# A fused linear attention and highway layer on one core: one written list of steps in place of a list scheduler, with the bias laid into PSUM by ScalarE and part of the blend on GpSimd

## The chip, the cores and the metric

The kernel runs on one core of one Trainium2 chip. The metric is the device time of one execution in microseconds (us), lower is better. Every time is a median of several executions; executions of one kernel mostly agree within a few per cent, and a run over 1.5% above the fastest of the same kernel is set aside as slow. A ratio is the mean time of one kernel's fast runs over the mean of the other kernel's fast runs of the same rounds on the same chip, so it is not quite the ratio of the medians quoted beside it; its 95% interval follows in brackets. The engines are TensorE (PE in the profile; its weight loads, PEld, run beside it), VectorE (DVE), ScalarE (ACT), GpSimd (POOL) and SyncE (SP), which here only issues transfers.

## The reference, cut to what matters

```python
# q, k, v: (8 batches, 8 heads, 576 rows, 64), float32; weights 512x512; output (4608, 512)
q_s = exp(q - max(q, -1));  q_s = q_s / sum(q_s, -1)        # softmax along the head dimension
k_s = exp(k - max(k, 2));   k_s = k_s / sum(k_s, 2)         # softmax along the sequence
kv  = einsum('bhsd,bhse->bhde', k_s, v)                     # 64x64 for each head
att = einsum('bhsd,bhde->bhse', q_s, kv)
x   = att.transpose(0, 2, 1, 3).reshape(4608, 512)
H   = maximum(x @ w_h, 0)
T   = sigmoid(x @ w_t + b_t)
out = T * H + (1 - T) * x
```

## The kernel before

Tokens go through in 36 tiles of 128 rows, four or five to a batch. For each batch: exponentials of k and q (ScalarE), casts of v, the product K'V (36 small matmuls per batch), its division by the sums, and transposes of exp(q) whose copies out of PSUM ("eq") feed the next product. For each tile: `xu` (product of eq and K'V), `x` (the division, VectorE), `xt` and `xe` (transposing x and copying it to SBUF), `mt` and `mh` (four 512-column matmuls each against the two weight matrices), `th` (tanh, ScalarE), `dd` and `uu` (the blend, VectorE), `oo` (the last addition, GpSimd) and two stores. w_h is halved and half of the identity taken from it beforehand, so that `mh` gives (x w_h - x)/2 and the blend is d = max((x w_h - x)/2, -x/2) and out = (tanh + 1) d + x, with tanh of half the T product.

What the change touches:

```python
    def mt(i, n, cols):                       # T product: four matmuls and a fifth for the bias
        ...
        if n < 4:
            nc.tensor.matmul(ps, T[f"xT{i}"][:, n], wt16[:, n, cols], start=(n == 0), stop=False,
                             skip_group_check=True)
        else:
            nc.tensor.matmul(ps, ones, b16[:, cols], start=False, stop=True, skip_group_check=True)
    ...
    def uu(i, cols):
        ...
        nc.vector.scalar_tensor_tensor(
            T[f"u{i}"][:, cols], T[f"tps{i}"][:, cols], 1.0, T[f"d{i}"][:, cols], op0=ALU.add, op1=ALU.mult)

    def oo(i, cols):
        ...
        eng = nc.vector if i == last else nc.gpsimd
        eng.tensor_add(T[f"o{i}"][:, cols], T[f"u{i}"][:, cols], T[f"x{i}"][:, cols])
    ...
    def wcast_h(c):                           # gate weights, on GpSimd in four pieces
        nc.gpsimd.tensor_scalar_mul(wh16[:, c], T["w32h"][:, c], 0.5)
```

All steps are entered into a list scheduler with an assumed length for each kind; it simulates the engines, buffers and loads and emits the instructions in the order that comes out.

The softmax here doesn't subtract the row's maximum and nothing guards it: scores larger than these inputs give would overflow.

## Time and profile before

The time was 137.18 us (136.13 to 138.89, 3 runs).

| engine | busy us of 134.7 | share |
|---|---|---|
| TensorE | 118.4 | 88% |
| VectorE | 104.4 | 77% |
| ScalarE | 88.5 | 66% |
| GpSimd | 63.1 | 47% |

TensorE idles 0.24 us between 40 and 121 us. Three more lines, from the groups of instructions by line and shape, are used later. The columns are line, engine, operation, output and input, shapes, count, then busy time in us and the mean of one in ns, then the idle time before them and what ended it:

```profile
L551 POOL TENSOR_TENSOR o<-u,x 128x512 f32<-128x512 f16 x35 | 40.4, 1155 | 43.9 <-DVE u L544 29.3 <-DMA out_dram<-o 5.1 <-DVE rz L402 4.6
...
L544 DVE SCALAR_TENSOR_TENSOR u<-tps,d 128x512 f16<-128x512 f32 x35 | 24.1, 688 | 2.8 <-ACT xT L515 0.5
...
L525 PE MATMUL tps<-b,ones 128*128 128x512 f16 x35 | 13.5, 386 | 0.0
```

All full-size output additions are on GpSimd at 1155 ns, VectorE's part of the blend takes 688 ns, and the bias matmul shows 386 ns.

The K'V products are good milestones, since there is one per batch and TensorE runs them in order. Three of them in the timeline of before (start us, length, engine, line, operation):

```profile
44.04 1.21 PE L391 MATMUL kv<-v,ek 64*128 64x130 f16 x36
67.06 1.21 PE L391 MATMUL kv<-v,ek 64*128 64x130 f16 x36
105.53 1.21 PE L391 MATMUL kv<-v,ek 64*128 64x130 f16 x36
```

### The profile page before, as it was taken

Reading aid. Unit: us, or ns where it says so; the run is one execution under the profiler, and the core shown is the slowest. Engines: PE = TensorE matmul, PEld = TensorE weight load, DVE = VectorE, ACT = ScalarE, POOL = GpSimd, SP = SyncE. Lnnn points to the kernel's source line nnn. Section 1 sums busy time; section 2 is a strip of 40 time slices with the busy share of each in tenths; the row PEclk is TensorE's granted clock in tenths of the full one; section 3 lists DMA queues with packets and bytes.
Section 4 is the critical chain, followed back from the end, with each engine's and each line's share of the span. In section 5 each row is a group of like instructions: output and inputs, shape, how many; then the busy total and the mean of one; then the engine's idle time right before and its main releaser. Section 6 shows DMA issues by size and latency. Waiting matters only on the chain.

```text
span 134.7 us, 3213 instructions
## 1 busy us (share of the span) xinstructions
PE 118.4 (88%) x1179; PEld 73.4 (55%) x1179; DVE 104.4 (77%) x220; ACT 88.5 (66%) x131; POOL 63.1 (47%) x63
## 2 busy tenths in 40 slices
PE   4778758879599999999999999999999999999920
PEld 4666533536255656665666575656665756555500
DVE  5566535999869798878989897879898977996760
ACT  3345464478885997979857979977697467444320
POOL 3011049536374349428833682495339516435430
PEclk9999986999999999999999999999999999999995
DMA  3999999999999999999999999999993341223234
GB/s 72 377 391 386 374 370 392 380 387 365 337 389 400 392 399 400 394 332 367 336 321 361 318 406 399 267 361 356 404 379 143 140 94 74 85 87 144 86 130 104
DMA packets 21011, 40.05 MB, mean 297 GB/s; under 512 B 1922, under 2 KB 4226, under 8 KB 20996
## 3 DMA queue, kind: packets, MB, share of 16 engines
q1 hardware_dynamic: 20832, 39.72, 82.5%
q8 instruction: 9, 0.15, 0.5%
q10 hardware_dynamic: 164, 0.14, 0.4%
q14 instruction: 6, 0.05, 0.1%
HBM read 30.41 MB, written 9.44 MB: 296 GB/s over the span
## 4 chain that ended last, share of the span: by engine, by line
PE 67%; DMA 15%; DVE 7%; POOL 5%; issue 2%; SPq 1%; DVEq 0%; POOLq 0%
PE tps L522 21%; PE gps L530 19%; DMA w32h<-in_moe_w_h_dram 10%; PE kv L391 6%; PE xu L491 6%; PE qps L445 5%; PE xtps L509 5%; PE tps L525 5%; DMA q<-in_q_dram 3%; POOL wh L326 3%; DVE u L544 2%; POOL o L551 2%; DMA out_dram<-o 2%; DVE x L502 2%; DVE d L539 1%
## 5 line engine op out<-in xcount | busy, mean ns | idle before, releaser
L551 POOL TENSOR_TENSOR o<-u,x 128x512 f32<-128x512 f16 x35 | 40.4, 1155 | 43.9 <-DVE u L544 29.3
L522 PE MATMUL tps<-wt,xT 128*128 128x512 f16 (+1 forms) x148 | 38.7, 379 | 1.4 <-ACT xT L515 0.8
L530 PE MATMUL gps<-wh,xT 128*128 128x512 f16 x144 | 38.2, 381 | 1.6 <-DVE wh L330 0.9
L515 ACT COPY xT<-xtps 128x512 f16<-128x512 f16 (+1 forms) x37 | 21.1, 571 | 15.6 <-PE xtps L509 15.5
L534 ACT ACTIVATE tps<-tps 128x512 f32<-128x512 f32 (+1 forms) x37 | 21.2, 572 | 12.2 <-PE tps L525 10.0
L544 DVE SCALAR_TENSOR_TENSOR u<-tps,d 128x512 f16<-128x512 f32 (+1 forms) x37 | 24.8, 674 | 3.7 <-ACT tps L534 1.0
L502 DVE TENSOR_TENSOR x<-xu,rs 128x512 f16<-128x512 f32 (+1 forms) x37 | 25.1, 678 | 3.3
L539 DVE SCALAR_TENSOR_TENSOR d<-x,gps 128x512 f16<-128x512 f16 x36 | 24.4, 679 | 2.7 <-PE gps L530 2.7
L374 POOL CAST v<-v 128x1152 f16<-128x1152 f32 (+1 forms) x16 | 16.4, 1026 | 15.0 <-DMA v<-in_v_dram 15.0
L436 ACT ACTIVATE qe<-q 128x1024 f16<-128x1024 f32 (+1 forms) x24 | 20.0, 840 | 3.8 <-DMA q<-in_q_dram 3.7
L366 ACT ACTIVATE ek<-k 128x1152 f16<-128x1152 f32 (+1 forms) x20 | 18.8, 967 | 3.5 <-DMA k<-in_k_dram 3.5
L522 PEld LDWEIGHTS <-xT 128*128 128x128 f16 x148 | 13.0, 99 | 12.5 <-issue 2.8
L530 PEld LDWEIGHTS <-xT 128*128 128x128 f16 x144 | 13.0, 99 | 10.8 <-issue 0.7
L491 PE MATMUL xu<-kvb,eq 128*128 128x130 f16 (+1 forms) x160 | 14.7, 226 | 1.3 <-DVE x L502 1.3
L491 PEld LDWEIGHTS <-eq 128*128 128x128 f16 (+1 forms) x160 | 10.8, 102 | 8.6 <-DVE x L502 3.0
L445 PE MATMUL qps<-idh,qe 128*128 128x128 f16 x144 | 12.2, 221 | 3.4 <-ACT qe L436 3.4
L509 PE MATMUL xtps<-idh,x 128*128 128x128 f16 x144 | 14.3, 221 | 0.2
L509 PEld LDWEIGHTS <-x 128*128 128x128 f16 x144 | 10.6, 98 | 6.7 <-DVE x L502 0.5
L525 PE MATMUL tps<-b,ones 128*128 128x512 f16 (+1 forms) x37 | 14.1, 380 | 0.0
L445 PEld LDWEIGHTS <-qe 128*128 128x128 f16 x144 | 9.4, 99 | 7.3 <-ACT qe L436 4.0
L498 DVE RECIPROCAL rs<-xu 128x8 f32<-128x8 f32 (+1 forms) x37 | 7.6, 204 | 6.8 <-PE xu L491 6.5
L457 ACT COPY eq<-qps 128x1024 f16<-128x1024 f16 x10 | 10.2, 1016 | 1.3 <-PE qps L445 1.3
(36 smaller groups left out, 79.4 us busy)
## 6 DMA issues: line engine op xcount, KB each, us to landing
k<-in_k_dram SPq DMA_DIRECT2D x16, 576.0 KB, 6.6
v<-in_v_dram SPq DMA_DIRECT2D x16, 576.0 KB, 7.7
out_dram<-o SPq DMA_DIRECT2D x70, 128.0 KB, 5.1
q<-in_q_dram SPq DMA_DIRECT2D x6, 1152.0 KB, 9.1
q<-in_q_dram SPq DMA_DIRECT2D x2, 640.0 KB, 12.0
q<-in_q_dram SPq DMA_DIRECT2D x2, 512.0 KB, 8.3
w32t<-in_moe_w_t_dram SPq DMA_DIRECT2D x2, 512.0 KB, 9.0
w32h<-in_moe_w_h_dram SPq DMA_DIRECT2D x2, 512.0 KB, 13.3
```

The lines of the kernel that those rows point to most:

```text
L445: nc.tensor.matmul(ps[:, j - j0, kk], T[f"qe{b}"][:, j, 2 * kk:2 * kk + 2].rearrange("p c d -> p (c d)"), idh, is_transpose=True, start=Tr ...
L491: nc.tensor.matmul(dst, T[f"eq{b}_{jp // 2}"][:, jp % 2, n], kvb[b % NKV][:, half_, kk], start=True, stop=True, skip_group_check=True)
L502: nc.vector.tensor_mul(T[f"xn{i}"][:, k0:k1], z[:, :, :, 0:64], r.unsqueeze(3).to_broadcast([P, k1 - k0, 4, D]))
L509: nc.tensor.matmul(T[f"xtps{i}"][:, n], T[f"x{i}"][:, n * P:(n + 1) * P], idh, is_transpose=True, start=True, stop=True, skip_group_check= ...
L515: nc.scalar.copy(T[f"xT{i}"][:, 2 * k0:2 * k1], T[f"xtps{i}"][:, 2 * k0:2 * k1])
L522: nc.tensor.matmul(ps, T[f"xT{i}"][:, n], wt16[:, n, cols], start=(n == 0), stop=False, skip_group_check=True)
L525: nc.tensor.matmul(ps, ones, b16[:, cols], start=False, stop=True, skip_group_check=True)
L530: nc.tensor.matmul(T[f"gps{i}"], T[f"xT{i}"][:, n], wh16[:, n], start=(n == 0), stop=(n == 3), skip_group_check=True)
L534: nc.scalar.activation(T[f"tps{i}"][:, cols], T[f"tps{i}"][:, cols], AF.Tanh, scale=0.5)
L539: nc.vector.scalar_tensor_tensor(d, T[f"x{i}"], -0.5, T[f"gps{i}"], op0=ALU.mult, op1=ALU.max)
L544: nc.vector.scalar_tensor_tensor(T[f"u{i}"][:, cols], T[f"tps{i}"][:, cols], 1.0, T[f"d{i}"][:, cols], op0=ALU.add, op1=ALU.mult)
L551: eng.tensor_add(T[f"o{i}"][:, cols], T[f"u{i}"][:, cols], T[f"x{i}"][:, cols])
```

## The change

The scheduler goes; a string with every step in order takes its place, and each step may name its engine (`:A` ScalarE, `:D` VectorE, `:P` GpSimd). Within this list: the bias of 26 tiles is copied into PSUM by ScalarE from a tile that holds it on all rows (`ball`), so that the T product adds to it; the product of 12 tiles' blend goes to GpSimd, which then makes two of its operations (`ee`, `uu`), while these tiles' or others' output additions, 12 in all, go to VectorE; w_h is loaded first and cast by VectorE; and tile 4's x is made in two halves as tile 0's was. The cut diff:

```diff
-class Plan:
-    ...                                  # the list scheduler, its lengths and its rules
+ORDER = """
+b_0 b_32 setuppool k_0_0 v_0_0 q_0_0 fill_24 half v_0_2 setupdve k_0_2 w_h_0 q_0_4 w_h_2 bsplit ek_0_0 ek_0_1 ball
+w_t_0 vc_0_1:A vc_0_0:D w_t_2 eq_0_0 v_1_0 fill_35 qt_0_0 kv_0_0 qc_0_0 bw_1 q_1_0 vc_0_2:D ek_0_3 kr_0_0 ek_0_2
+...
+    HALVED = (0, 4)
+...
+    def load_ball(e):
+        nc.scalar.dma_start(ball, moe_b_t.rearrange("(o n) -> o n", o=1).broadcast_to([P, DM]))
+...
+    def wh_cast(e, c):
+        nc.vector.tensor_scalar_mul(w16["h"][:, c:c + 2], w32["h"][:, c:c + 2], 0.5)
+...
+        if e == "A":
+            nc.scalar.copy(t, ball)
+        else:
+            nc.tensor.matmul(t, ones, b16, start=True, stop=False, skip_group_check=True)
+...
+        if lifted(i):
+            T[f"e{i}"] = dp.tile([P, DM], FP16, tag="e16", name=f"e16_{i}")
+            nc.gpsimd.tensor_add(T[f"e{i}"], T[f"d{i}"], T[f"x{i}"])
+...
+        if lifted(i):
+            nc.gpsimd.tensor_mul(t, T[f"th{i}"], T[f"d{i}"])
+        else:
+            nc.vector.scalar_tensor_tensor(t[:, cs], T[f"tps{i}"][:, cs], 1.0, T[f"d{i}"][:, cs],
+                                           op0=ALU.add, op1=ALU.mult)
+...
+        eng = nc.vector if e == "D" or i == LAST else nc.gpsimd
+        eng.tensor_add(t[:, cs], T[f"u{i}"][:, cs], T[f"{'e' if lifted(i) else 'x'}{i}"][:, cs])
```

The intent is to take the bias off the busiest engine, to spread the blend over VectorE and GpSimd, and to fix by hand an order that the scheduler's assumed lengths could not find.

## The prediction

> **What bounds the kernel now.** I read the page first, then the chain that ended last, then stretches of the timeline, to see whether the busiest engine is also the one whose order sets the end. From the page (40 slices of 3.37 us):
>
> ```profile
> span 134.7 us, 3213 instructions
> PE 118.4 (88%) x1179; PEld 73.4 (55%) x1179; DVE 104.4 (77%) x220; ACT 88.5 (66%) x131; POOL 63.1 (47%) x63
> ...
> PE   4778758879599999999999999999999999999920
> ...
> DVE  5566535999869798878989897879898977996760
> ...
> DMA  3999999999999999999999999999993341223234
> GB/s 72 377 391 386 374 370 392 380 387 365 337 389 400 392 399 400 394 332 367 336 321 361 318 406 399 267 361 356 404 379 143 140 94 74 85 87 144 86 130 104
> ```
>
> TensorE is full from slice 12 (40 us) to the tail, VectorE is near full beside it, and the DMA engines are full until about 101 us. The stretch 40 to 121 us, in the order busy PE, PEld, DVE, ACT, POOL, then granted clock, DMA share, GB/s:
>
> ```profile
> 40.00:121.00 81.00, 80.76 (x809) 49.16 (x809) 69.85 (x138) 61.57 (x92) 42.87 (x38) 1.00 0.84 301
> ```
>
> TensorE idles 0.24 us of 81, at full clock; VectorE still has 11.2 us of idle. As the end of a busy TensorE is modelled, I take its real pace from start times in the timeline (start, length, engine):
>
> ```profile
> 100.53 1.03 PE L522 MATMUL tps<-wt,xT 128*128 128x512 f16 x4
> ...
> 101.39 0.38 PE L525 MATMUL tps<-b,ones 128*128 128x512 f16 x1
> ...
> 101.60 0.40 PE L491 MATMUL xu<-kvb,eq 128*128 128x130 f16 x4
> ```
>
> Four 512-column matmuls take 0.86 us, one bias matmul (L525) 0.21 to 0.22 us of TensorE's order, not its 0.38. Before 40 us something else rules. The chain (start, length, what) and one later line of the timeline:
>
> ```profile
> 5.65 13.01 DMA w32h<-in_moe_w_h_dram
> 18.74 4.42 POOL wh L326 x3
> 23.18 0.70 DVE wh L330
> 23.92 0.38 PE gps L530
> ```
> ```profile
> 32.40 0.69 PE L391 MATMUL kv<-v,ek 64*128 64x130 f16 x18
> ```
>
> The gate weights land last, GpSimd casts them at 1491 ns a piece, and TensorE finishes tile 0's H product only after 25 us; batch 1's second K'V is at 32.40 us.
>
> **What the Trainium skill says.** "TensorE: Matmul & The Clock Gate", section "Wait — 56ns, not 53.3ns?", gives 215.7 ns from start to start for warm 512-column matmuls; 0.86 us for four agrees, so I use 0.2157. "PSUM — Partial Sum Buffer", section "The four PSUM rules", says that ScalarE writes neither set nor clear the written bits, and a matmul without the first flag adds where the bit is set. So the copied bias is added to only because the first user of each of the two T banks (tiles 0 and 1) still is a TensorE bias matmul with the flag and no later product has it; the trace of before cannot show this. "SBUF — State Buffer", section "Who interferes with whom", says a VectorE instruction with two SBUF inputs contends with GpSimd's reads. The kernel before has just two such adds, in the tail (418 ns for 256 columns), with GpSimd idle, so it shows nothing; the change makes twelve more beside GpSimd. "VectorE: DVE Perf Modes", section "Mode 2×_2P — use both read ports for one tensor", gives fp32 tensor_scalar in SBUF twice the rate; the casts of v at 746 ns for 576 columns do not show it, the 164 ns of the 128-column scaled identity leaves it possible.
>
> **The change part by part.**
>
> *Bias.* 37 bias matmuls (two of them halves, so 36 full ones' worth) become 10; 26 tiles get a ScalarE copy. TensorE loses 26 x 0.2157 = 5.6 us. The work that TensorE must do, at its real pace: 292 products of T and H worth 288 full ones, 62.2 us; bias 7.8; 36 xu groups 8.8 (32 x 0.23 + 4 x 0.35); 144 transposes of x and 144 of q at 0.056, 16.2; K'V 9.4 (6 x 1.15 + 4 x 0.63). Sum 104.4 before, 98.8 after. TensorE's last matmul ends at 129.2 us, so 24.8 us of that are idle, cold or filling. With that waste unchanged the span would be 134.7 - 5.6 = 129.1.
>
> *Head.* The list loads w_h before w_t, casts both on VectorE in two pieces each (by 576 columns in 746 ns, 1024 take some 1.2 us, or 0.63 if the double rate holds), and does tile 0's H product first. Bytes up to the last weight are the same 5.6 MB plus 0.26 for the bias spread over all rows, so weights are complete near 19.5 us (before 18.7). But tile 0 no longer waits for 5.9 us of GpSimd casts: its blend should come near 23 us (before 28.43). Batch 1's inputs are in after 8.8 MB, at 2.3 + 8.8/0.383 = 25.3 us; its second K'V should run near 28 instead of 32.4. Gain of the head some 4 us, an estimate.
>
> *VectorE.* Out: 12 blends x 0.688 = 8.3. In: 12 output adds x 0.69 = 8.3 (from x at 692 ns, same size). In: xT copies of 6 tiles and two halves, 6 x 0.60 + 2 x 0.28 = 4.1 (interpolated between the 1221 ns and 282 ns PSUM copies). Copies of q: 6 + 8 small become 4 + 6 small, -3.0. Two v casts fewer, -1.5; weight casts +2.5 to 4.8. Net +2 to +5: 104.4 becomes 106 to 109 us.
>
> *ScalarE.* 26 x 0.58 = 15.1 in; 8 steps of xT out, -4.1; q copies +2.7; v casts +3.2; w_t casts -2.1: 88.5 becomes 103.
>
> *GpSimd.* 12 adds of 1.155 and the 5.9 us of weight casts out, 24 new ops (e and u of 12 tiles) at some 1.15 in, v casts -1.8: 63 becomes 69. Not a bound.
>
> *Finer x steps.* Tile 4 is now halved as tile 0 was, and reciprocals stand apart from their products in the list; two more instructions each. This only matters at the start of batch 1 and is in the head's estimate.
>
> **What ends it: three bounds close together.** TensorE with the head's gain: 129.1 - 4 = 125. DMA: the last load of before is a v half issued at 94.38 us, cast by GpSimd at 101.88, and batch 7's K'V starts at 105.53. In the list 36 of the 74 stores stand before the last load (before: 42 of 74), so 30.4 + 0.26 + 36 x 0.131 = 35.4 MB must move first. At 383 GB/s (mean of slices 2 to 17) that is 92 us, at 370 (slices 2 to 30) 96; with 2.4 us to start, the last k lands at 95 to 98, its exponential (1.16 us) and handover bring K'V of batch 7 to 97 to 100. After it the list has 19 products of 4 (16.4 us), 7 xu (1.8), 7 xt (1.6), 12 transposes of q (0.7), one bias and K'V itself (1.4): 21.9 us, say 22.5 with small gaps, and the tail from the last matmul to the end is 5.5 us in before. That makes 125 to 128. VectorE: 107 us of work; it idled 9.3 us in the first 20 and 6.5 us after 121, which little can shorten, and 4 us more must be lost between: 127. With three lists that must mesh at 82 to 86% each, I take a span of 127.7. The median of before lies 2.5 us over its profiled span, so **130.2 us**, 5% less.
>
> **Rivals.** (a) *The bias was hidden, VectorE or the DMA binds and the time stays.* For: VectorE has 8 to 9 tenths nearly everywhere. Against: TensorE's 0.24 us idle in 81, where VectorE had 11 us free. If VectorE keeps those 11 us of idle with 3 us more work, the span is about 134 and the time 136. (b) *The shared SBUF port stretches the 12 adds and GpSimd's 24 ops:* up to one GpSimd op (1.15 us) per add on VectorE is 12 x 1.15 = 14 us at worst, a third of it likely if it happens at all; then near 132 to 134. (c) *A fixed order stalls:* with q, T, H and x buffers of one or two, one late copy on ScalarE (82% busy now) holds TensorE and lets its clock fall, as at 20 to 30 us (0.88). Against: the order looks made for just this, with xu two tiles ahead. Worth +2 us. (d) *The head gains its full 7 us* (TensorE wasted 7.2 us of 20 to 40) and the DMA keeps 395: 127.
>
> **Range and chances.** (d) sets the low end near 126.5, (b) with (c) the high end near 134. Only (a) or the worst of (b) keeps it above 134.4, the line of 2%; 5.6 us off the engine that was full for 81 us speaks strongly against. Faster by over 2%: 0.89; within: 0.10; slower: 0.01.
>
> **What would show it.** Right: 10 bias matmuls and 26 ScalarE copies of some 0.58 us; tile 0's blend near 23 us; K'V of batch 7 at 97 to 100; TensorE's last matmul near 122; VectorE near 107 busy, ScalarE near 103. Wrong: TensorE idle over some 4 us between 40 and 115 us with VectorE named as releaser (a); adds on VectorE or ops on GpSimd well over 0.69 and 1.15 us (b); granted clock under 0.97 after 40 us (c); DMA share well under 0.95 before the last load, so that TensorE waits at K'V.

## The result, and the profile after

The changed kernel took 131.11 us (130.32 to 133.31) against 137.02 for before in the same rounds, a ratio of 0.9589 [0.9502, 0.9676]: 4% faster. The profile read here is that of the control run e0_after, the same kernel again (131.53 us, span 129.7). The lines that answer to those of the page of before:

```profile
span 129.7 us, 3132 instructions
PE 113.2 (87%) x1170; PEld 71.5 (55%) x1170; DVE 105.2 (81%) x228; ACT 100.1 (77%) x156; POOL 71.6 (55%) x69
...
PE   4949379986999989999999999999998999999910
...
DMA  4999999999999999999999979999998450462453
```

TensorE has lost 5.2 busy us, ScalarE has gained 11.6, and TensorE is now full from slice 11 (32 us) on, with dents in slice 15 (45 to 49 us) and slice 31 (97 to 101 us). The DMA row keeps its nines to about 97 us, with one dent in slice 24 (75 to 78 us). The stretch of 40 to 121 us (busy PE, PEld, VectorE, ScalarE, GpSimd, each with its count, then granted clock, DMA share, GB/s), with a part of it:

```profile
40.00:60.00 20.00, 19.19 (x217) 11.79 (x216) 18.26 (x35) 18.95 (x30) 10.33 (x10) 1.00 1.05 390
...
96.00:102.00 6.00, 5.47 (x66) 3.68 (x65) 4.33 (x10) 5.48 (x10) 4.56 (x5) 1.00 0.77 286
...
40.00:121.00 81.00, 79.25 (x801) 47.59 (x800) 72.90 (x144) 74.61 (x117) 59.44 (x50) 1.00 0.85 306
```

TensorE still bounds this stretch, but idles 1.75 us in it where before idled 0.24. Nearly half of that, 0.81 us, lies between 40 and 60 us, where ScalarE is busy 18.95 of 20 us; another 0.53 at 96 to 102 us, around the last K'V. What TensorE waited for in the whole stretch (us in total, times, longest; waits too short to be named are left out):

```profile
PE qps L273 <- ACT eq L282: 0.4, 1, 0.4
PE gps L354 <- ACT xT L332: 0.3, 1, 0.3
PE xu L303 <- ACT eq L282: 0.3, 1, 0.3
PE turned L325 <- DVE x L318: 0.2, 1, 0.2
PE kv L238 <- ACT ek L224: 0.2, 1, 0.2
PE kv L238 <- DVE x L318: 0.2, 1, 0.2
```

So 1.2 us are put down to ScalarE and 0.4 to VectorE. The groups of the moved work:

```profile
L385 POOL TENSOR_TENSOR u<-th,d 128x512 f16<-128x512 f16 x12 | 15.2, 1267 | 1.6 <-ACT th L368 1.6
L338 ACT COPY tps<-ball 128x512 f32<-128x512 f32 x26 | 15.1, 593 | 0.5 <-DVE u L387 0.3
L379 POOL TENSOR_TENSOR e<-d,x 128x512 f16<-128x512 f16 x12 | 14.6, 1218 | 5.8 <-DVE d L374 5.7
...
L394 DVE TENSOR_TENSOR o<-u,x 128x512 f32<-128x512 f16 x6 | 7.0, 1172 | 0.1
...
L394 DVE TENSOR_TENSOR o<-u,e 128x512 f32<-128x512 f16 x6 | 5.4, 893 | 0.7 <-DMA out_dram<-o 0.7
...
L340 PE MATMUL tps<-b,ones 128*128 128x512 f16 x10 | 3.8, 380 | 0.0
```

The counts are as predicted. The additions on VectorE are not: they take 1172 and 893 ns in the mean, not 690. Asked for that line alone, the trace gives for the second of these groups a shortest, middle and longest duration of 684, 690 and 1469 ns. One by one, six of the twelve take 676 to 693 ns and six take 1141 to 1619. What sets them apart: each of the six long ones began while GpSimd was in the middle of an operation, and of the six short ones five did not (the sixth began 0.1 us before GpSimd's operation ended). It works the other way round too: eight GpSimd operations of 128x512 began inside one of these additions and take 1153 to 1597 ns, the 38 others after 25 us at most 1161. VectorE's `d` and `x`, with only one input in SBUF, began 48 times inside a GpSimd operation and never took over 692 ns. One long and one short addition, with the GpSimd operations beside them:

```profile
61.32 1.15 POOL L379 TENSOR_TENSOR e<-d,x 128x512 f16<-128x512 f16 x1
61.55 1.47 DVE L394 TENSOR_TENSOR o<-u,e 128x512 f32<-128x512 f16 x1
...
69.10 0.68 DVE L394 TENSOR_TENSOR o<-u,e 128x512 f32<-128x512 f16 x1
69.26 1.54 POOL L379 TENSOR_TENSOR e<-d,x 128x512 f16<-128x512 f16 x1 [0.58 <-DVE d L374]
```

The K'V milestones:

```profile
29.84 0.69 PE L238 MATMUL kv<-v,ek 64*128 64x130 f16 x18 [0.51 <-DVE rz L247]
41.53 1.21 PE L238 MATMUL kv<-v,ek 64*128 64x130 f16 x36
64.44 1.22 PE L238 MATMUL kv<-v,ek 64*128 64x130 f16 x36 [0.16 <-DVE x L318]
101.55 1.21 PE L238 MATMUL kv<-v,ek 64*128 64x130 f16 x36 [0.17 <-ACT ek L224]
```

To see where the time went I counted, from the order of the instructions, the TensorE work that stands ahead of each K'V at the real pace that the prediction uses (0.2157 us for a 512-column matmul and so on; an estimate), and subtracted it from the start. The rest is time that TensorE has wasted up to there: idle, at a low clock, or filling.

| K'V of batch | before: start, work, wasted | after: start, work, wasted |
|---|---|---|
| 1, second half | 32.40, 12.1, 20.3 | 29.84, 10.8, 19.0 |
| 2 | 44.04, 21.2, 22.9 | 41.53, 20.7, 20.9 |
| 4 | 67.06, 43.8, 23.3 | 64.44, 41.6, 22.9 |
| 7 | 105.53, 81.2, 24.4 | 101.55, 77.0, 24.6 |

At batch 1 and 2 the changed kernel is ahead by 1.3 to 2.0 us of waste, which is the gain of the head. By batch 7 this lead is gone. It went into the waits between: the 1.75 us of idle time from 40 to 121 us instead of 0.24. What is left is only that there is less work, 4.2 us less at this point and 5.6 at the end by the prediction's sum, and the span is 5.0 us shorter.

### The profile page after: what moved, and what is told of

Same layout as the page of the kernel before. It is cut to its first block, busy times and chain, and to the rows that moved or that the text cites.

```text
span 131.5 us, 3132 instructions
## 1 busy us (share of the span) xinstructions
PE 113.7 (86%) x1170; PEld 71.7 (55%) x1170; DVE 104.6 (80%) x228; ACT 100.3 (76%) x156; POOL 71.6 (54%) x69
## 4 chain that ended last, share of the span: by engine, by line
PE 38%; DMA 33%; ACT 12%; DVE 9%; issue 4%; DVEq 0%; SPq 0%; ACTq 0%
DMA q<-in_q_dram 16%; PE tps L348 12%; PE gps L354 12%; DMA k<-in_k_dram 11%; DMA ball<-in_moe_b_t_dram 6%; PE kv L238 4%; PE xu L303 4%; PE turned L325 4%; ACT ek L224 3%; ACT tps L370 3%; PE qps L273 3%; ACT qe L265 3%; DVE o L394 2%; DVE u L387 2%; ACT xT L332 2%
## 5 line engine op out<-in xcount | busy, mean ns | idle before, releaser
L348 PE MATMUL tps<-w16t,xT 128*128 128x512 f16 (+1 forms) x148 | 37.0, 373 | 0.1
L354 PE MATMUL gps<-w16h,xT 128*128 128x512 f16 x144 | 36.9, 379 | 0.3 <-ACT xT L332 0.3
L394 POOL TENSOR_TENSOR o<-u,x 128x512 f32<-128x512 f16 x17 | 19.6, 1155 | 19.6 <-DVE u L387 12.9
L224 ACT ACTIVATE ek<-k 128x1152 f16<-128x1152 f32 (+1 forms) x20 | 18.7, 966 | 7.8 <-DMA k<-in_k_dram 7.8
L387 DVE SCALAR_TENSOR_TENSOR u<-tps,d 128x512 f16<-128x512 f32 (+1 forms) x25 | 16.5, 662 | 4.3 <-ACT tps L370 3.4
L332 ACT COPY xT<-turned 128x512 f16<-128x512 f16 (+1 forms) x30 | 17.1, 571 | 2.4 <-PE turned L325 2.4
L370 ACT ACTIVATE tps<-tps 128x512 f32<-128x512 f32 (+1 forms) x25 | 14.1, 565 | 4.1 <-PE tps L348 2.5
L379 POOL TENSOR_TENSOR e<-d,x 128x512 f16<-128x512 f16 x12 | 14.6, 1218 | 4.1 <-ACT tps L370 2.8
L385 POOL TENSOR_TENSOR u<-th,d 128x512 f16<-128x512 f16 x12 | 15.2, 1271 | 1.3 <-ACT th L368 1.3
L325 PE MATMUL turned<-idh,x 128*128 128x128 f16 x144 | 14.3, 219 | 1.7 <-ACT xT L332 1.2
L338 ACT COPY tps<-ball 128x512 f32<-128x512 f32 x26 | 15.1, 591 | 0.5 <-DVE u L387 0.3
L282 ACT COPY eq<-qps 128x1024 f16<-128x1024 f16 x12 | 12.1, 1012 | 2.7 <-PE qps L273 2.6
```

Of the source, the lines that this page charges most:

```text
L224: nc.scalar.activation(t[:, :, c:c + n].rearrange("p j c d -> p c j d"), T[f"k32{b}"][:, c:c + n].rearrange("p c (j d) -> p c j d", j=NJ), ...
L325: nc.tensor.matmul(t[:, n], T[f"x{i}"][:, n * P:(n + 1) * P], idh, is_transpose=True, start=True, stop=True, skip_group_check=True)
L332: copy(t[:, 2 * k0:2 * k1], T[f"xtps{i}"][:, 2 * k0:2 * k1])
L348: nc.tensor.matmul(T[f"tps{i}"][:, cs], T[f"xT{i}"][:, n], w16["t"][:, n, cs], start=False, stop=(n == 3), skip_group_check=True)
L354: nc.tensor.matmul(t, T[f"xT{i}"][:, n], w16["h"][:, n], start=(n == 0), stop=(n == 3), skip_group_check=True)
L370: nc.scalar.activation(src, src, AF.Tanh, scale=0.5)
```

## The experiments

Twelve kernels ran, all correct, in three calls; the kernel before took 136.96, 137.31 and 136.01 us in them (medians, 11 runs each). A call keeps to one chip and has its own runs of before. I began with two theories of why the gain was below the prediction's by about a microsecond. Theory L: the last batch's loads come late, so that K'V of batch 7 and the tail hang on the DMA. Theory P: TensorE's own work sets the pace nearly everywhere. Against both stands a third way: the fixed order itself stalls.

| run | what | median us (range) | ratio to before | span of its profile |
|---|---|---|---|---|
| e0_after | the changed kernel | 131.39 (129.98–133.67) | 0.9574 [0.9514, 0.9634] | 129.7 |
| e1_bias_pe | all bias on TensorE | 134.96 (134.00–135.56) | 0.9857 [0.9805, 0.9909] | 132.7 |
| f1_before_seed | before, 26 biases by ScalarE | 134.45 (134.02–135.47) | 0.9840 [0.9786, 0.9894] | 133.7 |
| e3_loads_first | last loads ahead of stores | 136.56 (133.99–139.38) | none: one fast run | 134.6, slow |
| e2_blend_back | GpSimd's blend back, all additions to GpSimd | 135.51 (133.57–136.99) | 0.9852 [0.9770, 0.9933] | 132.4 |
| e4_first_bufs | e3 with 10 output buffers | 132.23 (131.44–133.22) | 0.9704 [0.9645, 0.9763] | 130.1 |
| e5_bufs | after with 10 output buffers | 131.71 (130.68–133.01) | 0.9651 [0.9583, 0.9718] | 128.9 |
| e6_head_old | old order and cast of the weights | 139.27 (138.45–140.63) | 1.0206 [1.0132, 1.0280] | 138.1 |
| e7_tile4_whole | tile 4's x in one piece | 132.24 (131.74–132.95) | 0.9723 [0.9676, 0.9770] | 130.3 |
| e8_blend_dve | GpSimd's blend to VectorE, additions stay | 133.39 (133.17–133.94) | 0.9803 [0.9762, 0.9845] | 132.1 |
| e9_batch7_first | all late loads early, 10 output buffers | 131.22 (130.69–131.43) | 0.9635 [0.9594, 0.9676] | 128.9 |
| e10_ball_late | the spread bias loaded later | 129.99 (129.54–131.77) | 0.9562 [0.9499, 0.9625] | 127.8 |

e0, e1, f1 and e3 ran in the first call, e2, e4, e5 and e6 in the second, the others in the third. Times of different calls are compared by their ratios to before.

**e0_after, the control.** The kernel unchanged.

> The changed kernel once more, as the control of this call and for a profile in the fast state. All theories: 130.3 to 131.5 us, ratio 0.95 to 0.96. Theory L (the late loads set the end): also in the fast state the DMA rate falls below 300 GB/s somewhere between 66 and 84 us while the load queue stands behind stores of tiles 9 to 13, and K'V of batch 7 starts no earlier than 100 us after a wait of TensorE. Rival P (TensorE's order alone sets the end): TensorE idles less than 1 us between 84 and 104 us.

It took 131.39 us, and gave the fast profile shown above. It shows the small idle time of TensorE after 60 us, which the slow profile had hidden: theory L has at most the 0.53 us at 96 to 102 us to live on. The signs of both theories came: the DMA rate fell to 211 GB/s in slice 24, and TensorE idled 0.53 us between 84 and 104 us.

**e1_bias_pe, the bias back on TensorE.**

```diff
-... bw_3:A ... bw_4:A ... (26 steps)
+... bw_3 ... bw_4 ...
```

> The list as it is, with the bias of all 36 tiles back on TensorE (26 more matmuls of 0.2157 us, 26 ScalarE copies of 0.59 us fewer). Rival P: TensorE pays all of it, 5.6 us more than the control. Theory L: only the 9 bias matmuls behind K'V of batch 7 cost their full 1.9 us, the 17 before it partly fill waits that are there anyway: 2 to 4 us more than the control, about 133 to 135 us. If ScalarE (76% busy) had become the bound: no change or a little faster.

It took 134.96 us against 131.39, so the bias is worth 3.6 us within the list (3.9 by the means of the fast runs alone), less than the 5.6 of TensorE's work that it removes. The same stretch of its profile:

```profile
60.00:121.00 61.00, 61.00 (x594) 36.07 (x592) 52.73 (x107) 46.04 (x68) 48.09 (x40) 1.00 0.79 278
40.00:121.00 81.00, 80.44 (x808) 48.08 (x807) 70.87 (x141) 62.38 (x92) 58.28 (x49) 1.00 0.85 304
```

With the bias, TensorE never stops after 60 us and idles 0.56 us of the 81. Without it, 1.75: the others, ScalarE with 74.61 us in this stretch instead of 62.38, do not quite keep up, and 1.2 us of what was gained returns as short waits (e1 has one named wait there, 0.3 us, against the six listed above); the other 0.8 of the 2.0 missing are outside this stretch and within what single profiles differ by. And 2.0 us (1 - 0.9857, of 137) remain for all the other parts of the change together, the spread bias, which e1 still loads though it no longer reads it, among them. In its profile these are a matter of the head: the second K'V of batch 1 starts at 29.62 us, 2.8 before that of the kernel before; from there to K'V of batch 7 it takes 73.18 us against 73.13, and from there to the end 29.9 against 29.2.

**f1_before_seed, the bias moved within the old kernel.** The scheduler stays; the same 26 tiles get a ScalarE copy as a scheduled step.

```diff
+    ball = consts.tile([P, DM], FP32, name="ball")
+    SEEDED = set(range(36)) - {0, 1, 2, 8, 11, 12, 13, 16, 22, 35}
...
+        add("ball", "ACT", "small", -10 ** 6 + 64, ..., lands=680)   # ahead of the other loads
...
-            for n in range(5):
+            for n in range(n_mt(i)):                                  # 4 if i in SEEDED, else 5
...
+    def bw(i):
+        T[f"tps{i}"] = ps_t.tile([P, DM], FP32, tag="tps", name=f"tps_{i}")
+        nc.scalar.copy(T[f"tps{i}"], ball)
```

> The kernel before with its list scheduler, and only the bias of the same 26 tiles laid into PSUM by ScalarE. If the bias alone gives the gain: about 131 us (ratio 0.955). My theory: TensorE gets 5 us of room but the last v of batch 7 lands near 101 us in the old order, so K'V of batch 7 moves from 105.5 to about 103 and only the bias behind it counts in full: 132 to 134 us (ratio 0.965 to 0.98). If the old scheduler cannot use it: 136 us or more.

The gain was 1.6%, 2.2 us. Its head came out worse: its second K'V of batch 1 starts at 34.52 us, 2.1 later than in before, and the last at 105.72. So this run is not the bias alone, and its small gain does not say that the bias is worth only 2.2 us. Two things can have made the head worse, and the run does not part them: the scheduler planned anew from the first step on, and the spread bias was issued at 1.51 us, ahead of most loads; batch 0's two halves of k land 1.0 and 1.2 us later than in before. Its TensorE, too, idles 1.78 us between 40 and 121 us (79.22 busy of 81), with ScalarE at 73.64 us there. But these are not the control's waits: the named ones, 1.5 us, are all put down to VectorE's `x`.

**e3_loads_first, the loads that came late moved ahead of stores.** In the list, stores and loads share SyncE's queue, and a store that waits for its addition holds up the loads behind it. The edit in words, eight steps of the list moved:

```diff
+ v_6_2 v_6_0 directly after k_5_2; k_6_0 k_6_2 after the stores of tile 11; q_6_0 after those of tile 12;
+ v_7_0, k_7_2, q_7_0 after those of tiles 14, 15 and 16     (before: from one to three tiles later)
```

> The list with eight loads of batches 6 and 7 placed ahead of the stores of tiles 9 to 17 that they stood behind, nothing else. Theory L: the DMA queue no longer runs dry near 72 to 80 us, K'V of batch 7 starts at 98 to 100 us, and the time is 127.5 to 129.5 us, 1.5 to 3 us under the control. Rival P: within 0.7 us of the control. A third way: the stores now land later, the five output buffers come free later, GpSimd waits for them, and it is slower by 1 us or more.

It seems to have got slower: all but one of its runs (133.99 us) were slow, so no ratio is given; the fast one is some 3 us above the control's fast runs. Its profile is slow, so I take from it only what another run confirms. A line of its timeline, with the idle time before it and its releaser in brackets:

```profile
98.13 1.16 POOL L394 TENSOR_TENSOR o<-u,x 128x512 f32<-128x512 f16 x1 [4.84 <-DMA out_dram<-o]
```

GpSimd stood 4.84 us at one addition because no output buffer was free: the stores now went out later. Its casts of v stand behind that addition. There are 5 output buffers, so the early stores in the list have a use: they free the buffers. The next run checks this.

**e5_bufs and e4_first_bufs, 10 output buffers.** The edit is one number; e5 has it on the changed kernel, e4 on e3.

```diff
-    op = pool("op", 5)
+    op = pool("op", 10)
```

> The changed kernel with ten output buffers, order unchanged. In the control's profile GpSimd waited 2.5 us and VectorE 0.7 us for stores, so output buffers are no limit there: within 0.7 us of the control (ratio 0.952 to 0.962). If buffers alone explain a gain of the version with the loads first, this one shows the same gain.

> The loads ahead of the stores once more, with ten output buffers in place of five. The version with five was slower because VectorE waited 3.5 us and GpSimd 8.4 us for stores to free an output buffer. If that was the whole of it: those waits vanish, K'V of batch 7 starts at 97 to 100 us and the time is 127 to 129.5 us (ratio 0.93 to 0.945). If the batch 6 loads still crowd out what TensorE needs at 78 us: 131 us or more.

e5 took 131.71 and e4 132.23 us in the same rounds, with overlapping intervals. The buffers heal e3's loss, as far as its one fast run shows a loss, so the loss was theirs; but the earlier loads bring nothing on top.

**e9_batch7_first, the strongest test of theory L.** All the loads that were left at the store of tile 14 go ahead of it.

```diff
-    op = pool("op", 5)
+    op = pool("op", 10)
- v_6_0 ... st_14 ... k_6_0 ... st_15_0_0 ... k_6_2 ... st_15_0_1 ... q_6_0 ... v_7_0 ... k_7_2 ... q_7_0 ... v_7_2 ... k_7_0
+ v_6_0 k_6_0 k_6_2 q_6_0 v_7_0 k_7_2 v_7_2 k_7_0 q_7_0 ... st_14 ... st_15 ...
```

> All loads that were left at the store of tile 14 (batch 6's k and q, batch 7 whole) stand before the stores of tiles 14 to 17, with 10 output buffers so that no add waits for a store. Batch 7's last k should land some 4 to 8 us earlier than 100.3 us. If late loads set the end: 1.5 us or more faster than the kernel after (ratio to before under 0.948). If TensorE's own work sets it, as its idle time of under 1 us between 60 and 120 us says: 0 to 0.8 us faster, ratio 0.951 to 0.958, K'V of batch 7 at 100.5 to 101.5 as before with no wait for the exponential.

The last k is issued at 79.62 instead of 89.53 us and lands 12.6 us later, at 92.2; in the control its exponential starts at 100.33, directly after the landing. Now neither the exponential nor K'V waits for anything named:

```profile
79.62 0.55 SPq L183 DMA_DIRECT2D k<-in_k_dram  x1
...
99.57 1.17 ACT L224 ACTIVATE ek<-k 128x1152 f16<-128x1152 f32 x1
100.86 1.21 PE L238 MATMUL kv<-v,ek 64*128 64x130 f16 x36
```

Eight microseconds of earlier data moved K'V by 0.7 us at most (e5, with the buffers alone, has it at 100.71) and the time not measurably: the ratio, 0.9635, lies between the controls of the other calls (0.9574 and, with buffers, 0.9651). Theory L falls for the fast state. The exponential simply stands at that place in ScalarE's order.

**e2_blend_back, the blend of 12 tiles off GpSimd.** The `ee` steps make nothing any more, the `uu` of these tiles run on VectorE, and all output additions on GpSimd, as in before. No step changes its place in the list.

```diff
     def ee(e, i):
-        ...
-            nc.gpsimd.tensor_add(T[f"e{i}"], T[f"d{i}"], T[f"x{i}"])
+        pass
...
-            nc.gpsimd.tensor_mul(t, T[f"th{i}"], T[f"d{i}"])
+            nc.vector.scalar_tensor_tensor(t, T[f"th{i}"], 1.0, T[f"d{i}"], op0=ALU.add, op1=ALU.mult)
...
-... oo_9_0:D ...        # and eleven more additions
+... oo_9_0 ...
```

> The GpSimd part undone: the 12 blends run on VectorE (one op of two SBUF inputs, the tanh still goes to SBUF), the 12 additions e fall away, and all output adds but the last tile's are on GpSimd. GpSimd 71.6 to about 56 us busy, VectorE 105.2 to about 102. If GpSimd's load is what held the stores and through them the loads (DMA dip at 72 to 84 us): the dip shrinks and the time falls 1 to 2.5 us under the control (131.4 in the call before, ratio 0.957). If the blending on GpSimd earns its keep by freeing VectorE: 1 to 3 us slower. If neutral: within 0.7 us.

By ratio it lost 2.0% against e5 of the same call (0.9852 to 0.9651), but its timeline shows that most of this is no cost of the blend:

```profile
43.85 1.21 PE L238 MATMUL kv<-v,ek 64*128 64x130 f16 x36 [2.65 <-POOL v L230]
```

TensorE stood 2.65 us at K'V of batch 2 for a cast of v on GpSimd. The output addition of tile 4, now on GpSimd, stands ahead of that cast in the list. K'V of batch 2 is 2.3 us later than in the control and K'V of batch 7 still 2.0 later. Between the two e2 takes 59.67 us and the control 60.02: with blend and additions both back on the engines where before had them, e2 loses nothing over these five batches. Its loss is that one wait and 0.7 us after the last K'V (28.9 us instead of 28.2). So the run tested the place of an addition in a list more than the blend.

**e8_blend_dve, the blend moved to VectorE, with the twelve additions left there too.**

```diff
         if lifted(i):
-            nc.gpsimd.tensor_mul(t, T[f"th{i}"], T[f"d{i}"])
+            nc.vector.scalar_tensor_tensor(t, T[f"th{i}"], 1.0, T[f"d{i}"], op0=ALU.add, op1=ALU.mult)
...
-        eng.tensor_add(t[:, cs], T[f"u{i}"][:, cs], T[f"{'e' if lifted(i) else 'x'}{i}"][:, cs])
+        eng.tensor_add(t[:, cs], T[f"u{i}"][:, cs], T[f"x{i}"][:, cs])
```

> A cleaner undo of the move to GpSimd: the product of the 12 lifted tiles goes to VectorE (one instruction on two SBUF tiles, some 0.7 us), the e additions fall away, the output adds stay on the engines where the list has them. VectorE gets 12 x 0.7 = 8.4 us more (105 to 113 busy), GpSimd 24 operations (some 29 us) less, and with them the stretched adds on VectorE should fall from 0.98 to about 0.7 us. Theory V (VectorE is a second bound close behind TensorE, so the move was needed): 3 to 6 us slower than the kernel after, ratio to before 0.98 to 1.00, TensorE waits named for VectorE. Theory T (TensorE alone binds between 40 and 120 us and VectorE's idle and the freed port absorb it): within 1 us, ratio 0.95 to 0.965.

The control did not run in this call. By ratios e8 lies 2.3% above it, 3.1 us of 136; by medians 2.2 us above e9, which ran in the same rounds and which by its ratio is within a per cent of the changed kernel. So with the additions on VectorE, it is worth 2 to 3 us that GpSimd makes the blend: at the lower edge of theory V or just under it, and clearly not nothing, so theory T falls. This prices one half of an exchange: before has neither the additions on VectorE nor the blend on GpSimd, and e2, which undoes both, shows no loss from K'V of batch 2 to that of batch 7. That the exchange as a whole gains anything there is not shown. The stretch as above, and one wait:

```profile
40.00:121.00 81.00, 77.09 (x784) 45.49 (x783) 75.57 (x152) 73.16 (x113) 28.57 (x25) 1.00 0.85 303
```
```profile
72.62 0.41 PE L303 MATMUL xu<-kvb,eq 128*128 128x130 f16 x4 [1.52 <-DVE x L318]
```

VectorE has 2.7 us more work in the stretch, TensorE loses 2.2 us more than in the control, and 1.5 of them are one wait for VectorE's x. Also, the additions on VectorE are only partly freed: the group takes 839 ns in the mean and the blend on two SBUF tiles 802, with longest durations of 1626 and 1351, as GpSimd still adds and casts beside them.

**e7_tile4_whole, the finer x steps undone.**

```diff
-    HALVED = (0, 4)
+    HALVED = (0,)
- xu_4_0 ... rs_4_0 ... x_4_0 xu_5_0 ... xu_4_1 ... rs_4_1 x_4_1 ... xt_4_1 ... xe_4_1 ... mt_4_1 ... mh_4_1
+ xu_4_0 rs_4_0 x_4_0 xu_5_0 ...
```

> Undo of the finer x steps alone: tile 4's x is made, turned and copied in one piece, at the place of its second half. If the finer steps are worth something it is the start of batch 1's products: TensorE idled there 0.4 to 0.8 us in the kernel after, so up to 0.7 us slower (ratio to before 0.957 to 0.963). If they are worth nothing: 0.957 within 0.006. Only if another engine's fixed order runs onto the later x, as in the earlier runs, more than 1 us slower.

(The whole x was built at the place of the first half and not of the second, as the expectation has it.) It took 132.24 us, 1.0 above e9 in the same rounds, more than I expected. Three waits at the start of batch 1's tiles in its timeline, where the control has a single one, of 0.68 us:

```profile
31.64 0.41 PE L303 MATMUL xu<-kvb,eq 128*128 128x130 f16 x4 [0.54 <-DVE kvb L255]
33.07 0.41 PE L303 MATMUL xu<-kvb,eq 128*128 128x130 f16 x4 [1.03 <-DVE x L318]
38.00 0.41 PE L303 MATMUL xu<-kvb,eq 128*128 128x130 f16 x4 [0.69 <-DVE x L318]
```

That is 2.26 us of waits instead of 0.68, and K'V of batch 2 starts at 42.58 instead of 41.53. The 1.03 us are a wait for the x of the tile before: whole tiles share the one `xu` buffer, while halved ones write into the two buffers of the H product. So the finer x steps are worth about 1 us, by ratio to the control's up to 2 (0.9723 to 0.9574).

**e6_head_old, the head's order and the cast of the weights undone.** w_t before w_h, and GpSimd casts w_h in four pieces.

```diff
- ... w_h_0 q_0_4 w_h_2 ... w_t_0 ... w_t_2
+ ... w_t_0 q_0_4 w_t_2 ... w_h_0 ... w_h_2
-        nc.vector.tensor_scalar_mul(w16["h"][:, c:c + 2], w32["h"][:, c:c + 2], 0.5)
+        for c1 in (c, c + 1):
+            nc.gpsimd.tensor_scalar_mul(w16["h"][:, c1], w32["h"][:, c1], 0.5)
```

> The start undone: w_t loaded before w_h as in the kernel before, and w_h cast by GpSimd in four pieces (1.2 to 1.5 us each), all else as in the changed kernel. My predicted gain of the head was 4 us. If the late loads decide the end, part of it is lost again: tile 0's blend moves from 23 to 27 or 28 us, second K'V of batch 1 from 29.8 to 32 to 34 us, and the time rises by 1 to 3 us. If the head's gain carries to the end in full: 4 us or more. If it is all hidden behind the loads: under 0.7 us.

It lost 8 us, far beyond what I expected, and was slower than before. Two lines of its timeline:

```profile
19.37 5.85 POOL L209 TENSOR_SCALAR w16h<-w32h 128x512 f16<-128x512 f32 x4 [17.57 <-DMA w32h<-in_moe_w_h_dram]
...
24.13 2.51 PE L168 MATMUL turned<-idh 128*128 128x128 f16 x22 [5.53 <-DVE xT L333]
```

GpSimd's casts take 5.85 us, as they did in before. But here the steps of the diagonal, which wait for them, stand in VectorE's list ahead of the x and xT of tiles 0 and 1, which do not. VectorE runs in order, so it waits, TensorE waits 5.53 us for xT, its granted clock over 20 to 40 us falls to 0.80, and K'V of batch 1 comes at 37.59. The scheduler of before had put other work there. The cast is therefore not worth 8 us as such; with a list, a step that is late at one place holds all that is written after it.

**e10_ball_late, the spread bias out of the head.** The profile of the control showed an unexpected thing: the second half of batch 0's k, issued at 2.80 us, lands at 13.2 us, and ScalarE, which was to take its exponential, waited 3.91 us for it. The 0.26 MB of the spread bias were issued at 4.64 us from ScalarE's queue.

```diff
- ... ek_0_0 ek_0_1 ball w_t_0 ... vc_0_3:A ...
+ ... ek_0_0 ek_0_1 w_t_0 ... vc_0_3:A ball ...
```

> The bias spread over all rows (0.26 MB) is loaded after the first v's casts instead of ahead of the gate weights; its first reader is tile 3. If the head is bound by bytes up to the weights: 0.26 MB at 0.38 MB per us = 0.7 us earlier weights, up to 0.7 us faster (ratio 0.952 to 0.957). If it only shares queues with loads that aren't urgent: the same as the kernel after within 0.3 us.

It took 129.99 us, 1.2 less than e9 in the same rounds. First two lines of the control's timeline, then those that answer to them in that of e10, with two of its K'V:

```profile
13.19 1.26 ACT L224 ACTIVATE ek<-k 128x576 f16<-128x576 f32 x2 [3.91 <-DMA k<-in_k_dram]
...
20.30 1.28 DVE L203 TENSOR_SCALAR w16t<-w32t 128x1024 f16<-128x1024 f32 x2
```
```profile
11.20 0.69 ACT L224 ACTIVATE ek<-k 128x576 f16<-128x576 f32 x1 [1.96 <-DMA k<-in_k_dram]
...
19.74 0.69 DVE L203 TENSOR_SCALAR w16t<-w32t 128x1024 f16<-128x1024 f32 x1 [0.49 <-DMA w32t<-in_moe_w_t_dram]
...
28.18 0.69 PE L238 MATMUL kv<-v,ek 64*128 64x130 f16 x18 [0.51 <-POOL v L230]
...
99.60 1.21 PE L238 MATMUL kv<-v,ek 64*128 64x130 f16 x36 [0.18 <-ACT ek L224]
```

The exponential comes 2 us earlier than in the control, K'V of batch 1 at 28.18 instead of 29.84 (in the other profiles of the list with the early spread bias, e6 aside, it lies between 28.99 and 30.01), K'V of batch 7 at 99.60 instead of 101.55, and the span is 127.8 instead of 129.7 (128.9 in e5 and e9). The control is the slowest but one of these profiles in the head: against all ten, K'V of batch 1 gains 0.8 to 1.8 us, 1.3 in the mean. The lead is kept to the end: by the count used above, K'V of batch 7 has 22.6 us of waste ahead of it instead of 24.6. As a time, e10 is the fastest kernel, and well ahead of before. Against the changed kernel itself it did not run in the same rounds: by ratios to before (0.9562 and 0.9574) the two cannot be told apart, by the neighbour e9 and by its profile it is 1 to 2 us faster. That part stays open.

## Why the prediction was right or wrong

The predicted 130.2 us were 0.9 below the measured 131.11, and the range held it. Step by step:

**TensorE is the bound: right.** It is busy 79.25 us of 81 after the change, and giving it the bias back costs 3.6 to 3.9 us (e1).

**Bias, 5.6 us: right in the work, too high in the time.** Ten bias matmuls and 26 copies of 593 ns are there, and TensorE's end came from 129.2 to 123.6 us (its last matmuls start at 122.56 and take 1.04). What failed is "with that waste unchanged": without the bias matmuls TensorE idles 1.75 us in the stretch from 40 to 121 us, with them 0.56 (e1), and the net is 3.6 to 3.9 us.

**Head, some 4 us: the mechanism right, the size wrong.** Tile 0's blend comes at 23.67 us, as predicted. But the second K'V of batch 1 came at 29.84, not near 28. (Of the 2.6 us gained there, the table gives 1.3 to less waste.) The term that was mis-sized is "plus 0.26 for the bias spread over all rows", which I priced by its bytes at 0.7 us. e10 shows that its place in the head cost some 1.3 us at that K'V (0.8 to 1.8 against the single profiles) and 1.1 us of time by the means of the fast runs of e9 and e10; without it K'V comes at 28.18 and the span, 127.8, is the predicted 127.7. Two limits: no run parts the new order of the loads from the new engine of the casts, so how the gain of the head divides between them is not shown; and the "18.7" of the text is where the first half of w_h lands in before, the second half landing at 20.03 us. The last weight lands at 20.63 in the control, so against before the weights themselves came 0.6 us later, near the 0.7 of the price by bytes. The step "Finer x steps ... in the head's estimate" stood without a number; e7 measures about 1 us.

**VectorE 106 to 109 us: it has 105.2, just below.** The 12 additions cost 12.4 us (7.0 + 5.4) instead of 8.3, the xT copies 3.1 (six of 416 ns and two of 285) instead of 4.1, and the steps of the diagonal, which the text left out, 1.1 instead of 2.4. The casts of the weights take 2.7, because the double rate does hold. Added up one by one, VectorE's durations grew by 3.7 us (110.9 to 114.7), inside the text's 2 to 5; the busy time, which counts overlapping instructions once, grew by only 0.8. That VectorE is a second bound close behind was right: when its busy time rose by 5.3 us in e8, the kernel lost 2 to 3 us.

**ScalarE 103, GpSimd 69: near, at 100.1 and 71.6.** That ScalarE has become the engine that TensorE waits for between 40 and 60 us stood in the text only as rival (c), a late copy on ScalarE.

**The DMA as third bound: wrong.** The last k landed at 100.31 us, later than the "95 to 98" of the text, and K'V of batch 7 at 101.55 is later than its "97 to 100". But the one did not make the other: with the data there 8 us earlier (e9) K'V still came at 100.86 and the time stayed, while a faster head alone (e10) brought K'V to 99.60. The argument "the last load, then 21.9 us of work" holds only if TensorE comes to that point too early, and it does not.

**Rivals.** (a), that the bias was hidden, fell with e1. (b), the shared port, is right in the mechanism: VectorE's additions and GpSimd's operations hold each other up one by one, as shown above, and the additions are stretched by 4.1 us in sum, near the third of 14 us that the text thought likely. The time of 132 to 134 us that it drew from this did not come; no run takes away the contention alone, so its cost in time stays open. (c), stalls of a fixed order, is true in the size given, of the order of 1.5 us in the changed kernel, though the clock that it saw falling stayed at 1.00 from 40 to 121 us, and it is far more where I edited the list: 2.65 us in e2, 5.53 in e6. (d) did not come.

So of the 7 us that the prediction gave (134.7 to 127.7 in span, 137.2 to 130.2 in time), 5.9 came by the medians of the same rounds. The two profiled spans show only 5.0, because the profile of before was a quick execution (136.47 us) and that of e0 a slow one (131.53): in every run the time lies 1.7 to 1.9 us over its own span, and the 2.5 us that the prediction added hold 0.7 for the quick draw. The spread bias in the head, 1.1 us of time, is as large as the rest. That e10 meets the number is partly luck: the text took its last 2.6 us of loss from the DMA and VectorE as bounds, and the runs show short waits for ScalarE and VectorE in their place.

## What to carry to other kernels

Taking work off a full engine returns the whole of it only as long as the other engines have time left where it was. Here 3.6 to 3.9 us of 5.6 came back, beside a ScalarE that was busy 18.95 us of 20. And an undo prices only what it undoes: e8 left half of an exchange in place and lost 2 to 3 us, e2 undid both halves and lost most of its time at a single wait. Such prices do not add up to the whole.

Price a small transfer in the head by what it delays and not only by its bytes: two thirds of a microsecond of bytes cost 1.1 us of time, and it went out beside a load that an early exponential was waiting for.

A written list is as good as its assumptions: after any edit, look first for the in-order queue in which a late step now stands ahead of an urgent one, before saying what the edited part itself costs.

## What the Trainium skill lacked or had wrong

- "SBUF — State Buffer", section "Who interferes with whom": that a VectorE operation with two SBUF inputs contends with GpSimd's reads is borne out: an operation that began inside one of the other engine's was stretched, in both directions. The page gives the loser's wait no size for such mixed work; here 128x512 additions that take 676 to 693 ns undisturbed took 1141 to 1619, and GpSimd's operations of the same shape, at most 1161 undisturbed, up to 1597.
- "PSUM — Partial Sum Buffer", section "🎯 Summary: rules for kernel authors": it says that a seed by ScalarE must be 0. With a bias that is not 0, copied by ScalarE into banks whose bits an earlier matmul had set and no later first flag cleared, all eleven kernels that do this were correct; the rule by bits in the page's section "The four PSUM rules" is the one to go by.
- "VectorE: DVE Perf Modes", section "Mode 2×_2P — use both read ports for one tensor": agrees for fp32 tensor_scalar, 687 ns for 1024 columns. The casts of v, 748 ns for 576 columns in a rearranged pattern, do not reach it; no run tests whether the page's condition on the outermost dimension is why.
- "DMA: Bandwidth & Descriptors", section "Queues, rings and completion order", describes how queues take turns on a DMA engine, but neither it nor another page has a number for what a small load of one row spread over 128 rows does to other loads in flight. Here 0.26 MB of it, issued 1.8 us after a load of 0.59 MB, went with a landing of that load 0.9 to 2.0 us later (eleven profiles, 12.08 to 13.17 us) than without it (11.18). No run tells whether the second queue, the pattern or the moment makes this.
